# Spectral stages of a two-layer kernel: casts out of one PSUM bank put side by side on ScalarE, a tail copy moved ahead of the sums, differences split by columns, the last filter groups sent from three queues

## The chip, the cores and the metric

The kernel runs on one core of one Trainium2 chip. A core has five engines that each work through their own list of instructions in order: TensorE (PE; its weight loads are listed apart as PEld), VectorE (DVE), ScalarE (ACT), GpSimd (POOL) and SyncE (SP). They wait for each other by semaphores. Transfers (DMAs) are started by an instruction on the list of SP, ACT or POOL and then run by themselves. PSUM is the memory into which TensorE writes its sums; SBUF is the memory that all engines work in; DRAM is the chip's large memory. The metric is the device time of one execution in microseconds (us).

## The reference

A 2048 x 576 array x goes through four residual blocks, A, B, A, B. A is sliding-window attention with 32 heads; the change leaves it alone. B multiplies the two-dimensional spectrum of the normalised array by a filter:

```python
def _B_ref(x, w_r, w_i):
    B, S, D = x.shape
    X = jnp.fft.rfft2(x, axes=(-2, -1))
    W = w_r + 1j * w_i
    X = X * W
    return jnp.fft.irfft2(X, s=(S, D), axes=(-2, -1))
...
x = x + _A_ref(_layernorm(x, axis=-1), A_wqkv, A_wo)
x = x + _B_ref(_layernorm(x, axis=-1), B_w_r, B_w_i)
x = x + _A_ref(_layernorm(x, axis=-1), A_wqkv, A_wo)
x = x + _B_ref(_layernorm(x, axis=-1), B_w_r, B_w_i)
```

## The kernel before

The two B blocks are two calls of `layer_b`, called the first and the second spectral layer below. Transforms are products with constant matrices. A float32 factor is mostly written as a high and a low part of a shorter type (fp32r): ScalarE casts a PSUM tile to the high part, VectorE subtracts this from the same PSUM tile for the low part, and TensorE multiplies high by high, high by low and low by high. Each layer runs three stages, each over 16 tiles.

**Stage f, the forward transform** (lines 195 to 259; helpers in class `Out`). The last product of the attention block is made here too, since both feed TensorE: for each token tile u, `out.ahead(u)` loads the tile, turns it (lines 566 to 579) and splits it (ScalarE cast of 512 columns, line 575; VectorE subtraction, line 576; the same for a last 128 columns, lines 587 and 588), `out.unit(u)` makes 28 matmuls (line 593) and adds the residual, `out.sums(u)` takes mean and variance. `f0(u)` normalises (ScalarE `xn`, line 198), folds the row into even and odd halves and splits a 33-column tail (GpSimd, lines 200 to 208). `f1` turns the folded tile into the PSUM tile `tp`, of which there is one, with ScalarE casts `et` (line 220) and `em` (line 222) and the VectorE subtraction between them (line 221); `f2` transforms along the row (14 matmuls, line 232; cast `yh`, subtraction `yl`), `f3` along 128 of the 2048 tokens (line 243), `f4` makes sum and difference (lines 249 to 251) and writes the tile `yd` to DRAM. The order is written out by hand: an opening (lines 273 to 287), a loop over t = 1 to 10 (lines 288 to 301), and an ending (lines 303 to 314). In the opening three tiles are normalised ahead, `norm(u)` being `sums` and `f0`; in the loop's first turn two `f0` follow each other (lines 300 and 301).

**Stage g, the filter** (lines 317 to 371). 16 groups g go through `pipe`, which in step t runs `g2(t-9)`, then `g1m(t-7)`. `g1m` makes 4 matmuls (line 331), multiplies the result by the filter on VectorE (lines 337 and 338) and combines the products on GpSimd (`uv`, lines 340 and 341). `g2` makes 4 matmuls of `uv` into `pq` (line 350) and needs the sum and the difference of the two halves of `pq`: in odd groups and in group 14 ScalarE copies one half (line 355) and VectorE makes both from PSUM (lines 356 and 357); in the other groups ScalarE copies both halves (line 359), VectorE adds (line 360) and GpSimd subtracts (line 361). The result goes to DRAM (`yd`, line 366) by ScalarE's queue (even groups and the odd ones up to 7) or by SyncE's. The last stage's first two tiles, `yis[0]` and `yis[1]`, don't wait for the way through DRAM of the last groups: groups up to FG - 1 = 11 are read back from DRAM (line 365), and groups 12 to 15 are also sent straight from SBUF, 8 rows each (line 369), by SyncE's queue, those of group 15 by ScalarE's. `warm(40)` (line 372) then keeps TensorE busy with 40 matmuls that nothing reads.

**Stage i, the inverse transform** (lines 375 to 434). `pipe` runs in step t: `ly(t)` and `ld(t-3)` (loads), `i1(t-4)`, `i2(t-5)`, `im(t-3)`, `i0(t-2)`. `i0` splits a tile into a high and a low z (ScalarE line 382, VectorE line 383), `im` copies 33 columns of each to a second place (line 388 on ScalarE, line 389 on VectorE), where the third column chunk of `i1` reads them. `i1` makes 18 matmuls into the PSUM tile `pi` (line 400; the last four of the wait below read the copied columns) and splits it: `zh`, `zl` from one bank, `zm` from the next (lines 406 to 409). `i2` makes 16 matmuls into `po` (lines 420 and 424); ScalarE copies its second half (`bs`, line 427), VectorE adds the residual twice (lines 428 and 429), GpSimd adds and subtracts `bs` (lines 430 and 431), SyncE writes the rows out. In the first spectral layer the next attention block's opening runs along in this stage (`next(nxt)`).

## Time and profile before

| | us |
|---|---|
| runs shown | 1498.57, 1501.96, 1508.23 |
| median | 1501.96 |
| the profiled execution | 1499.43 |
| its span, first to last instruction | 1497.7 |
| second spectral layer, stage f, from the first turn of tile 0 to the end of the last sums | 1230 to 1356 |
| second spectral layer, stage g | 1360 to 1405 |
| second spectral layer, stage i | 1410 to 1493 |

The times on the left of a timeline row are us from the span's start. A group row gives line, engine, operation, tile written <- tiles read, shapes and count, busy us, mean ns of one, and the idle time before it with what ended it. A wait row says which instruction waited for which, the sum in us, the count, and the longest. A windows row gives for each engine the busy us and count in a stretch, then PEclk (the granted TensorE clock as a share of full), the mean busy share of the DMA engines and GB/s. A tile is listed by the place it lies in: `oroom` and `ofree` are two large SBUF areas that hold z, the turned tiles, x and `yis`. The first spectral layer stands in the trace at 490 to 752 with the same rows.

### The profile page before, as it was taken

To read this page: it belongs to the slowest core of one execution; us is meant where nothing else is said; L and a number is where in the kernel's file an instruction comes from. 1 tells how busy PE (TensorE), PEld (TensorE's weight loads), DVE (VectorE), ACT (ScalarE), POOL (GpSimd) and SP (SyncE) were. 2 spreads that over 40 slices of the span, in tenths; PEclk is the share of its full clock that TensorE was granted. 3 is DMA by queue.
4 is the path that set the end of the run, shared out by engine and by line. 5 is a ranking of instruction groups with operands and counts; after the bars stand their busy time and mean duration, and the time that the engine had idled before them with its cause. 6 is when DMAs were issued, how large, how long until landed. Compare 5 with 4: busy or idle time off the path is not lost. (4 is left out here: it accounts for less than half of the span.)

```text
span 1497.7 us, 34567 instructions
## 1 busy us (share of the span) xinstructions
PE 1413.8 (94%) x11928; PEld 1068.9 (71%) x11928; DVE 957.0 (64%) x3140; ACT 819.5 (55%) x1994; POOL 689.2 (46%) x1134
## 2 busy tenths in 40 slices
PE   7999999999999899889899999999999988999887
PEld 7976666666656799658899766666666568985686
DVE  4328777777882565566752487777777735656575
ACT  5523777777785454224454257777777844542243
POOL 2266555555565432343321954545455644324333
PEclk9999999999999999999999999999999999999999
DMA  6756556556445475757664575665554354667553
GB/s 189 201 166 212 172 179 194 179 177 177 148 133 154 127 229 187 259 192 247 217 172 93 184 220 165 167 166 159 164 156 134 101 182 157 215 211 256 175 175 127
DMA packets 203220, 266.59 MB, mean 178 GB/s; under 512 B 103918, under 2 KB 109038, under 8 KB 202214
## 3 DMA queue, kind: packets, MB, share of 16 engines
q1 hardware_dynamic: 192934, 242.23, 53.2%
q10 hardware_dynamic: 7872, 15.70, 3.1%
q0 software_dynamic: 2240, 6.45, 1.6%
q8 instruction: 96, 1.57, 0.5%
q14 instruction: 78, 0.64, 0.1%
HBM read 165.58 MB, written 101.47 MB: 178 GB/s over the span
## 5 line engine op out<-in xcount | busy, mean ns | idle before, releaser
L895 DVE CUSTOM_DVE_ANT_0 jk<-S,mask 128x384 bf16<-128x384 f32 (+2 forms) x1024 | 490.6, 529 | 112.7 <-PE E L930 61.5
L931 ACT ACTIVATE P<-E 128x384 f32<-128x384 f32 (+2 forms) x1024 | 409.0, 476 | 124.0 <-PE E L930 102.8
L933 POOL TENSOR_SCALAR_AFFINE_SELECT P<-P 128x512 f32<-128x512 f32 x256 | 163.0, 637 | 278.5 <-ACT P L931 250.5
L893 PE MATMUL S<-ks,qs 63*128 63x384 f32 (+2 forms) x1024 | 269.1, 372 | 1.0 <-DMA qs<-qk_d 0.4
L930 PE MATMUL E<-qs,ks 64*128 64x384 f32 (+2 forms) x1024 | 222.4, 373 | 4.5 <-ACT P L931 2.5
L893 PEld LDWEIGHTS S<-ks,qs 63*128 63x128 f32 x1024 | 140.8, 185 | 105.5 <-DVE m L895 73.3
L950 PE MATMUL U<-P,vq 128*19 128x128 f32 (+1 forms) x3840 | 188.7, 329 | 1.0 <-ACT us L955 1.0
L836 PE MATMUL pj<-xh,wqh 128*128 128x512 f32 x360 | 156.6, 435 | 3.1 <-ACT vt L780 1.7
L950 PEld LDWEIGHTS U<-P,vq 128*19 128x19 f32 x3840 | 95.9, 98 | 78.0 <-issue 22.7
L936 POOL TENSOR_SCALAR_AFFINE_SELECT P<-P 128x512 f32<-128x512 f32 x224 | 142.7, 637 | 0.0
L593 PE MATMUL ops<-oroom 128*128 128x288 f32 x840 | 123.5, 303 | 4.4 <-DVE oroom L576 3.0
L930 PEld LDWEIGHTS E<-qs,ks 64*128 64x128 f32 x1024 | 114.1, 185 | 18.7 <-ACT P L931 9.2
L836 PE MATMUL pj<-xh,wql 128*128 128x512 f32 x360 | 124.5, 419 | 0.4 <-POOL wql L498 0.4
L836 PE MATMUL pj<-xl,wqh 128*128 128x512 f32 x288 | 122.2, 424 | 0.0
L593 PEld LDWEIGHTS ops<-oroom 128*128 128x128 f32 x840 | 115.3, 193 | 6.2 <-DVE oroom L576 4.0
L400 PE MATMUL pi<-oroom 128*128 128x128 f32 (+1 forms) x576 | 73.7, 277 | 21.0 <-DVE oroom L389 16.1
L836 PEld LDWEIGHTS pj<-xh,wqh 128*128 128x128 f32 x360 | 67.9, 189 | 34.7 <-issue 10.6
L400 PEld LDWEIGHTS pi<-oroom 128*128 128x128 f32 (+1 forms) x576 | 68.6, 192 | 25.9 <-DVE oroom L389 20.0
L851 DVE TENSOR_TENSOR sg<-pj,sg 128x512 fp32r<-128x512 f32 x72 | 49.5, 687 | 58.4 <-ACT sg L848 58.4
L895 DVE DVE_READ_ACCUMULATOR2_ANT m<- 128x1 f32 x1024 | 85.1, 83 | 0.0
L430 POOL TENSOR_TENSOR xo<-xo,bs 128x289 f32<-128x289 f32 x32 | 25.5, 798 | 123.9 <-DVE xo L428 123.9
L836 PEld LDWEIGHTS pj<-xh,wql 128*128 128x128 f32 x360 | 64.2, 189 | 21.0 <-issue 10.7
(186 smaller groups left out, 2604.6 us busy)
## 6 DMA issues: line engine op xcount, KB each, us to landing
qk_d<-sg SPq DMA_DIRECT2D x56, 512.0 KB
qs<-qk_d SPq DMA_DIRECT2D x384, 72.0 KB
ks<-qk_d SPq DMA_DIRECT2D x348, 72.0 KB
v_d<-vt SPq DMA_DIRECT2D x32, 304.0 KB
vq<-v_d SPq DMA_DIRECT2D x16, 608.0 KB
yd<-ye SPq DMA_DIRECT2D x32, 290.0 KB
wt<-in_w SPq DMA_DIRECT2D x16, 580.0 KB
x<-ofree SPq DMA_DIRECT2D x32, 288.0 KB
```

What stands on the lines that cost most here:

```text
L400: T.matmul(o, z[:, sl, c, lo:lo + m], mo, start=k == 0, stop=k == 2)
L430: P.tensor_add(xo[:, 0:DF], xo[:, 0:DF], bs[:, 0:DF])
L593: self.nc.tensor.matmul(self.ps[u][n][:, 0:288], x, self.w[p][:, wk * D + n * 288:wk * D + n * 288 + 288], start=first and i == 0, stop=la ...
L836: T.matmul(box["ps"].rearrange("r (n p) -> r n p", n=NT) if second else box["ps"], w[:, wk], x, start=s == 0, stop=s == len(ks) - 1)
L851: V.tensor_sub(rest[:, 1], by, rest[:, 0].bitcast(F32))
L893: T.matmul(ps[:, 0:N], q[b:b + 63, pair, i * 128:i * 128 + 128], k[b:b + 63, pair, lo:hi], start=True, stop=True)
L895: V.tensor_tensor_reduce(out=jk[:, 0:N], in0=ps[:, 0:N], in1=mask[:, 384 - N:384], scale=1.0, scalar=-3e38, op0=ALU.add, op1=ALU.max, accu ...
L930: T.matmul(ps[:, 0:nq], k[b:b + 64, pair, j * 128:j * 128 + 128], q[b:b + 64, pair, j * 128:j * 128 + nq], start=True, stop=True)
L931: A.activation(p[:, hl_, 0:nq], ps[:, 0:nq], AF.Exp, scale=SC)
L933: P.affine_select(out=p[:, :, 0:128], in_=p[:, :, 0:128], pattern=[[0, 4], [1, 128]], compare_op=ALU.is_ge, fill=0.0, base=0, channel_mult ...
L936: P.affine_select(out=p[:, :, 256:384], in_=p[:, :, 256:384], pattern=[[0, 4], [-1, 128]], compare_op=ALU.is_gt, fill=0.0, base=0, channel ...
L950: T.matmul(U[32 * h:32 * h + 19, (q0 % 4) * 128:(q0 % 4) * 128 + 128 * (q1 - q0)], vts[n][:, j, h], pt[n, j][:, h, (q0 - j) * 128:(q1 - j) ...
```

## The change

In stage f the cast `em` stands ahead of VectorE's subtraction for `et`, and the cast of the last 128 columns (in `turn`) ahead of the subtraction of the first 384: ScalarE's two casts of a PSUM tile follow each other, then VectorE's two subtractions. The turn of tile 5 stands ahead of `f2(0)`, the turn of tile 6 and the sums of tile 4 ahead of the loop, and each turn of the loop normalises tile t + 3 where it normalised t + 4, so none has two. In the ending, tile 15's first 22 matmuls stand first, its last 6 after `f1(11)` and `f3(10)`, and tiles 14 and 15 are normalised earlier among the f's.

In stage g every group but 15 is done alike: ScalarE copies both halves, VectorE adds, and of the difference GpSimd makes the first 192 columns and VectorE the other 98. FG is 11, so groups 11 to 15 are sent straight. Group 14's way to DRAM goes from ScalarE's queue to SyncE's, its two straight pieces and one of group 15's to GpSimd's queue; ScalarE keeps one piece of group 15.

In stage i the tail copy is one ScalarE instruction for both parts of z and stands ahead of `i2`; the cast `zm` stands ahead of the subtraction `zl`.

```diff
@@ -130,7 +130,7 @@
 
     yd = [dram.tile([16, 16, 8, 2 * NF], F32, name=f"yd{j}") for j in range(2)]
     OPEN = *range(7, 20, 2), 20
-    FD, FG = 13, 12
+    FD, FG, SH = 13, 11, 192
     with ExitStack() as stack:
         banks, inner = ExitStack(), ExitStack()
         ip = stack.enter_context(tc.tile_pool(name="bi", bufs=1))
@@ -218,8 +218,8 @@
             em = h["em"] = wp.tile([128, 2, 128], F32R, tag="te", name=f"em{n2}", bufs=3)
             t4 = tp[:, :, 0:256].rearrange("p c (a t) -> p c a t", a=2)
             A.copy(et[:, :, 0:2], t4)
+            A.copy(em[0:99], tp[0:99, :, 256:384])
             V.tensor_sub(et[:, :, 2:4], t4, et[:, :, 0:2].bitcast(F32))
-            A.copy(em[0:99], tp[0:99, :, 256:384])
 
         def f2(n2, h):
             ps = pp.tile([128, 2, 512], F32, tag="mm", name=f"pf{n2}", bufs=3)
@@ -281,36 +281,37 @@
         out.tail(6)
         f1(0, hs[0])
         out.unit(4, pp)
+        out.ahead(5, pp)
         f2(0, hs[0])
-        out.ahead(5, pp)
         norm(3)
         out.tail(7)
+        out.ahead(6, pp)
+        out.sums(4)
         for t in range(1, NT - 5):
             u = t + 4
             out.unit(u, pp)
             f1(t, hs[t])
             f3(t - 1, hs[t - 1])
             f4(t - 1, hs[t - 1])
-            if t == 1:
-                out.ahead(6, pp)
             out.sums(u)
             f2(t, hs[t])
             out.ahead(u + 2, pp)
-            if t == 1:
-                norm(4)
-            f0(u, hs[u])
+            f0(u - 1, hs[u - 1])
 
         b = NT - 1
-        for v, f in ((b - 4, f1), (b - 5, f3), (b - 5, f4), (b - 4, f2), (b - 3, f1)):
+        ps = pp.tile([128, 2, 512], F32, tag="mm", name="opsb", bufs=3)
+        out.early(b, [ps[:, 0], ps[:, 1]])
+        for v, f in ((b - 4, f1), (b - 5, f3), (b - 1, f0), (b - 5, f4)):
             f(v, hs[v])
-        out.unit(b, pp)
+        out.late(b)
         out.sums(b)
         for z in zs:
             V.memset(z.bitcast(F32)[:, :, :, 289:320], 0.0)
         nc.sync.dma_start(ic.rearrange("p a f -> p (a f)").bitcast(F32), ic_d.rearrange("p a f -> p (a f)").bitcast(F32))
         nc.sync.dma_start(ga.rearrange("p a j c -> p (a j c)").bitcast(F32), ga_d.bitcast(F32))
-        for v, f in ((b - 2, f1), (b - 3, f2), (b - 4, f3), (b, f0), (b - 4, f4), (b - 1, f1), (b - 2, f2), (b - 3, f3), (b - 3, f4),
-                     (b, f1), (b - 1, f2), (b - 2, f3), (b - 2, f4), (b, f2), (b - 1, f3), (b - 1, f4), (b, f3), (b, f4)):
+        for v, f in ((b - 3, f1), (b - 4, f2), (b, f0), (b - 2, f1), (b - 3, f2), (b - 4, f3), (b - 4, f4),
+                     (b - 1, f1), (b - 2, f2), (b - 3, f3), (b - 3, f4), (b, f1), (b - 1, f2), (b - 2, f3), (b - 2, f4),
+                     (b, f2), (b - 1, f3), (b - 1, f4), (b, f3), (b, f4)):
             f(v, hs[v])
         warm(24)
 
@@ -351,22 +352,24 @@
 
             ye = wp.tile([128, 2, NF], F32, tag="ye", name=f"ze{g}", bufs=3) if g % 2 else eos[g // 2 % 4]
             both = ip.tile([128, 2, NF], F32, tag="both", name=f"both{g}", bufs=2)
-            if g % 2 or g == 14:
+            if g == 15:
                 A.copy(both[:, 1], pq[:, 1, 0:NF])
                 V.tensor_add(ye[:, 0], pq[:, 0, 0:NF], both[:, 1])
                 V.tensor_sub(ye[:, 1], pq[:, 0, 0:NF], both[:, 1])
             else:
                 A.copy(both, pq[:, :, 0:NF])
+                P.tensor_sub(ye[:, 1, 0:SH], both[:, 0, 0:SH], both[:, 1, 0:SH])
                 V.tensor_add(ye[:, 0], both[:, 0], both[:, 1])
-                P.tensor_sub(ye[:, 1], both[:, 0], both[:, 1])
+                V.tensor_sub(ye[:, 1, SH:NF], both[:, 0, SH:NF], both[:, 1, SH:NF])
             yef = ye.rearrange("p c f -> p (c f)")
             if g == FG + 1:
                 for n2 in range(2):
                     nc.sync.dma_start(yis[n2][0:8 * FG].rearrange("p c f -> p (c f)"), yd[1][n2, 0:FG].rearrange("g i f -> (g i) f"))
-            (nc.sync if g % 2 and g > 8 else nc.scalar).dma_start(yd[1][:, g].rearrange("n i f -> i n f"), yef)
+            (nc.scalar if g < 13 and (g < 8 or g % 2 == 0) else nc.sync).dma_start(yd[1][:, g].rearrange("n i f -> i n f"), yef)
             if g >= FG:
                 for n2 in range(2):
-                    (nc.scalar if g == 15 else nc.sync).dma_start(yis[n2][8 * g:8 * g + 8].rearrange("p c f -> p (c f)"), yef.rearrange("(i n) f -> n i f", n=16)[n2])
+                    q = nc.sync if g < 14 else P if g == 14 or n2 else nc.scalar
+                    q.dma_start(yis[n2][8 * g:8 * g + 8].rearrange("p c f -> p (c f)"), yef.rearrange("(i n) f -> n i f", n=16)[n2])
 
         pipe(16, [(9, g2), (7, g1m), (2, gw), (0, g0)])
         warm(40)
@@ -385,8 +388,7 @@
         def im(n2, h):
             z = zs[n2 % 3]
             zf = z.bitcast(F32)
-            A.copy(z[:, 0, :, 320:353], zf[:, 0, :, 256:289])
-            V.tensor_copy(z[:, 1, :, 320:353], zf[:, 1, :, 256:289])
+            A.copy(z[:, :, :, 320:353], zf[:, :, :, 256:289])
 
         def i1(n2, h):
             z = zs[n2 % 3]
@@ -404,8 +406,8 @@
             zm = h["zm"] = ip.tile([128, 2, 128], F32R, tag="zm", name=f"zm{n2}", bufs=3)
             zhf, zlf, zmf = [a.rearrange("p a b n -> p (a b n)") for a in (zh, zl)] + [zm.rearrange("p b n -> p (b n)")]
             A.copy(zhf, psf[:, 0:512])
+            A.copy(zmf[0:97], psf[0:97, 512:768])
             V.tensor_sub(zlf, psf[:, 0:512], zhf.bitcast(F32))
-            A.copy(zmf[0:97], psf[0:97, 512:768])
             V.tensor_sub(zmf[64:97], psf[64:97, 512:768], zmf.bitcast(F32)[64:97])
 
         def i2(n2, h):
@@ -431,7 +433,7 @@
             P.tensor_sub(xo[:, 575:288:-1], xo[:, 575:288:-1], bs[:, 1:288])
             nc.sync.dma_start(dstv[:, n2], xo)
 
-        pipe(NT, [(0, ly), (3, ld), (4, i1), (5, i2), (3, im), (2, i0)], lambda t: t in OPEN and nxt and next(nxt))
+        pipe(NT, [(0, ly), (3, ld), (4, i1), (3, im), (5, i2), (2, i0)], lambda t: t in OPEN and nxt and next(nxt))
         share["banks"] = pp
         if nxt:
             next(nxt)
@@ -573,10 +575,12 @@
             T.transpose(last, self.o7[:, u], self.ident)
         copy = self.nc.vector.tensor_copy if e is self.nc.vector else self.nc.scalar.copy
         copy(oT[:, 0:512], tp)
+        oL = self.oL[u % 3]
+        if last is not None:
+            self.nc.scalar.copy(oL[:, 0:128], last)
         self.nc.vector.tensor_sub(oT[:, 512:896], tp[:, 0:384], oT[:, 0:384].bitcast(F32))
-
         if last is not None:
-            self.split_last(u, last)
+            self.nc.vector.tensor_sub(oL[:, 128:256], last, oL[:, 0:128].bitcast(F32))
 
     def turn_last(self, u, tp):
         self.nc.tensor.transpose(tp, self.o7[:, u], self.ident)
```

Three places show how the instructions stand. First, VectorE in one step of stage i, second spectral layer, before; the names are those above, `oroom<-oroom` is the tail copy and `oroom<-ofree,oroom` the low part of z:

```order
L407 TENSOR_TENSOR zl_21247<-pi_21227,zh_21246 128x512
L409 TENSOR_TENSOR zm_21248<-pi_21227,zm_21248 33x256
L428 TENSOR_TENSOR xo_21270<-ofree,po_21253 128x289
L429 TENSOR_TENSOR xo_21270<-ofree,po_21253 128x287
L389 CAST oroom<-oroom 128x2x33
L383 TENSOR_TENSOR oroom<-ofree,oroom 128x2x289
```

and a step after the change (its line numbers are those of the changed file):

```order
L410 TENSOR_TENSOR zl_21092<-pi_21072,zh_21091 128x512
L411 TENSOR_TENSOR zm_21093<-pi_21072,zm_21093 33x256
L430 TENSOR_TENSOR xo_21116<-ofree,po_21099 128x289
L431 TENSOR_TENSOR xo_21116<-ofree,po_21099 128x287
L386 TENSOR_TENSOR oroom<-ofree,oroom 128x2x289
```

The tail copy has left VectorE, where it stood behind the two additions that wait for `po`. On ScalarE it stands, after the change, between `zm` and `bs`:

```order
L408 CAST zh_21424<-pi_21405 128x512
L409 CAST zm_21426<-pi_21405 97x256
L391 CAST oroom<-oroom 128x4x33
L429 COPY bs_21450<-po_21432 128x290
L385 CAST oroom<-ofree 128x2x289
```

Second, ScalarE in the first two turns of stage f's loop, second spectral layer, from the casts of a turned tile of the attention product (`oroom<-tpo`) to the cast `et` of tile 2; before:

```order
L575 CAST oroom<-tpo_19246 128x512
L587 CAST oroom<-tpo_19246 128x128
L627 ACTIVATE ofree<-ofree,eps 128x1
L198 ACTIVATE xn_19262<-ofree 128x576
L201 COPY eo_18971<-xn_19262 128x2
L627 ACTIVATE ofree<-ofree,eps 128x1
L198 ACTIVATE xn_19274<-ofree 128x576
L201 COPY eo_18973<-xn_19274 128x2
L220 CAST et_19322<-tp_19315 128x2x256
```

and after the change:

```order
L577 CAST oroom<-tpo_19250 128x512
L580 CAST oroom<-tpo_19250 128x128
L631 ACTIVATE ofree<-ofree,eps 128x1
L198 ACTIVATE xn_19263<-ofree 128x576
L201 COPY eo_18972<-xn_19263 128x2
L220 CAST et_19311<-tp_19304 128x2x256
```

One normalisation stands ahead of `et` where two stood. Third, the end of stage g on ScalarE, second spectral layer, groups 12 to 15, before:

```order
L366 DMA yd_18956<-eo_18975 8x16x580
L355 COPY both_20871<-pq_20865 128x290
L355 COPY both_20896<-pq_20891 128x290
L366 DMA yd_18956<-eo_18977 8x16x580
L355 COPY both_20909<-pq_20903 128x290
L369 DMA ofree<-ze_20908 8x580 x2
```

and after the change:

```order
L368 DMA yd_18957<-eo_18976 8x16x580
L360 COPY both_20889<-pq_20883 128x580
L360 COPY both_20913<-pq_20908 128x580
L356 COPY both_20927<-pq_20921 128x290
L372 DMA ofree<-ze_20926 8x580
```

The transfer of group 14 (`eo_18977`) no longer stands between the copies of groups 14 and 15, and one of the two straight pieces is left. GpSimd's list, which ended with the two `uv` of group 15, now ends so:

```order
L361 TENSOR_TENSOR ze_20888<-both_20889 128x192
L341 TENSOR_TENSOR uv_20905<-ofree 128x290
L342 TENSOR_TENSOR uv_20905<-p_15_20902 128x290
L361 TENSOR_TENSOR eo_18978<-both_20913 128x192
L372 DMA ofree<-eo_18978 8x580 x2
L372 DMA ofree<-ze_20926 8x580
```

Three transfers now stand behind GpSimd's last subtraction.

## Prediction

> **What bounds the kernel now.** I read the busy row first, then stretches of the second spectral layer by stage, then what TensorE's weight loads waited for, then single steps in the timeline.

> ```profile
> PE 1413.8 (94%) x11928; PEld 1068.9 (71%) x11928; DVE 957.0 (64%) x3140; ACT 819.5 (55%) x1994; POOL 689.2 (46%) x1134
> 1310.00:1345.00 35.00, 33.32 (x239) 32.25 (x238) 19.05 (x52) 16.31 (x38) 8.39 (x21) 0.95 0.60 199
> 1367.00:1402.00 35.00, 33.55 (x224) 15.99 (x222) 29.12 (x51) 7.07 (x14) 24.68 (x35) 1.00 0.69 231
> 1414.00:1498.00 84.00, 68.05 (x524) 65.84 (x524) 52.32 (x93) 31.59 (x76) 26.91 (x32) 0.95 0.48 160
> ```

> TensorE carries the kernel. Where a spectral layer leaves it idle, as in 16 of the 84 us from 1414 (stage i), a wait that goes is time gained, until another engine's work per step reaches TensorE's. In stage g (1367 to 1402) TensorE shows 33.55 of 35 us and VectorE 29.12.

> **Stage i: the tail copy leaves VectorE.** Waits of the weight loads in the first layer's stage i (first row) and in the second's; then one step of the second:

> ```profile
> PEld pi L400 <- DVE oroom L389: 10.1, 14, 1.2
> PEld pi L400 <- DVE oroom L389: 9.9, 14, 1.0
> ...
> 1431.71 0.65 DVE L389 CAST oroom<-oroom 128x66 fp32r<-128x66 f32 x1
> 1432.41 0.42 PEld L400 LDWEIGHTS pi<-oroom 128*97 128x97 f32 x4 [0.99 <-DVE oroom L389]
> ...
> 1425.37 0.41 ACT bs L427
> ...
> 1483.15 0.41 ACT bs L427
> ```

> The copy of tile n + 1 stands behind VectorE's two additions for the `po` of tile n - 1, so TensorE stops in each step until these are through. The two `bs` rows of the chain lie 12 steps apart: 57.8 / 12 = 4.82 us a step. Of that 9.9 / 14 = 0.71 is this wait; 4.11 is TensorE's own work. After the change the copy stands on ScalarE behind `zm`, about two us before it is read. What is late next? VectorE had 52.32 us over some 17 steps, 3.1 a step, and loses 0.65; ScalarE 1.9, plus at most 0.3 for a longer copy; GpSimd 1.6: all under 4.11. L383, next in VectorE's list, is read by TensorE only a step later. So the wait goes, but not in the first steps, where z comes from transfers still: I take -9 per layer of 9.9 and 10.1. Bounds: 0.71 x 14 = -10, and -5 should half come back as a wait for `zl` or `zm`, whose subtraction now stands one cast (0.37 us) later; in the first layer VectorE also works for the next attention block.

> **Stage f: order of casts, one normalisation per turn, the ending.** In the loop's steady turns the moved cast costs and saves nothing: TensorE's list has no gap there and the low part, which now comes one cast later, is read only behind the eight matmuls of the high part. At the ends, waits of the weight loads from 1231 to 1357:

> ```profile
> PEld pf L232 <- ACT et L220: 3.4, 2, 2.2
> PEld ops L593 <- DVE oroom L576: 2.0, 2, 1.5
> PEld tp L214 <- POOL tl L208: 1.6, 1, 1.6
> PEld pz L243 <- DVE yl L236: 1.4, 2, 0.8
> PEld tpo L570 <- ACT em L222: 1.2, 1, 1.2
> PEld ops L593 <- ACT oroom L575: 0.9, 1, 0.9
> ```

> The order shows a remedy for each but the 1.5 of L576, which lies before the loop, and the 0.6 of L236 at the very end. `et` came behind two normalisations, now one; `f0(15)`, which makes `tl`, stands ahead of `f1(13)` where it stood behind `f3(11)`, with two tiles' f1, f2 and f3 before its reader; the turn of tile 6 has 2 us of `f2(0)` between it and the turn of tile 5. Gone: 3.4 + 0.5 + 1.6 + 0.8 + 1.2 + 0.9 = 8.4. New: the turn of tile 5 needs `tp` as soon as unit 4 ends:

> ```profile
> 1238.12 3.74 PEld L593 LDWEIGHTS ops<-oroom 128*128 128x128 f32 x28
> 1241.32 0.58 ACT L220 CAST et<-tp 128x512 fp32r<-128x512 f32 x1
> 1241.94 0.69 DVE L221 TENSOR_TENSOR et<-tp,et 128x512 fp32r<-128x512 f32 x1 [1.65 <-ACT et L220]
> 1242.66 0.37 ACT L222 CAST em<-tp 99x256 fp32r<-99x256 f32 x1 [0.76 <-DVE et L221]
> ```

> `tp` is free at 1241.90 + 0.37 + 0.69 = 1243.0 and TensorE is there at 1241.9: 1.1 us. Net -7 per layer. Bounds: -4, if half of the ending's waits come back, and -9, as the PEclk of 0.95 from 1310 to 1345 says 0.05 x 35 = 1.75 us go to a slower clock behind the ending's gaps.

> **Stage g: differences split.** Weight loads of `pq` in the second layer, four groups, and the instructions of one pair:

> ```profile
> 1372.27 0.79 PEld L350 LDWEIGHTS pq<-uv,m 64*128 64x128 f32 x8 [0.44 <-issue]
> 1374.58 0.79 PEld L350 LDWEIGHTS pq<-uv,m 64*128 64x128 f32 x8 [0.44 <-POOL uv L340]
> 1384.52 0.79 PEld L350 LDWEIGHTS pq<-uv,m 64*128 64x128 f32 x8 [0.44 <-issue]
> 1386.66 0.46 DVE L360 TENSOR_TENSOR eo<-both 128x290 f32<-128x290 f32 x1
> 1386.68 0.99 POOL L341 TENSOR_TENSOR uv<-p 128x290 f32<-128x290 f32 x1
> 1389.03 0.40 ACT L355 COPY both<-pq 128x290 f32<-128x290 f32 x1 [2.41 <-POOL uv L340]
> 1389.54 0.79 PEld L350 LDWEIGHTS pq<-uv,m 64*128 64x128 f32 x8 [0.44 <-issue]
> ...
> L360 DVE TENSOR_TENSOR eo<-both 128x290 f32<-128x290 f32 x7 | 4.1, 580 | 2.4 <-ACT both L359 2.3
> L389 DVE CAST oroom<-oroom 128x66 fp32r<-128x66 f32 x16 | 9.5, 591 | 0.1
> ...
> 1387.04 0.75 DVE L337 TENSOR_TENSOR ofree<-p,wt 128x580 f32<-128x580 f32 x1
> 1387.71 0.75 DVE L338 TENSOR_TENSOR p<-p,wt 128x580 f32<-128x580 f32 x1
> ```

> A group costs TensorE 2.31 (1372.27 to 1374.58) and takes 5.02 / 2 = 2.51 (1384.52 to 1389.54). At best 14 x 0.20 = -2.8 per layer. But each group now has two VectorE instructions that read SBUF alone beside GpSimd's three, and the rows show what such neighbours do: L360 began at 1386.66 and the `uv` beside it took 0.99. The short subtraction of 98 columns isn't in this trace; the nearest is L389, 591 ns mean. With L360's mean of 580 and twice 0.68 for L337 and L338 (they start 1387.71 - 1387.04 = 0.67 apart) a group costs VectorE 0.58 + 0.59 + 1.36 = 2.53, what it takes now: 0. Upper bound, all at their longest: 0.99 + 0.65 + 1.36 = 3.00, 15 x 0.49 = +7 per layer.

> [...]

> **From g to i: three queues.**

> ```profile
> 1403.04 5.37 PEld L265 LDWEIGHTS warm<-dc 128*128 128x128 f32 x40 [0.39 <-issue]
> 1403.43 0.58 ACTq L366 DMA_DIRECT2D yd<-eo  x1
> 1404.11 0.40 ACT L355 COPY both<-pq 128x290 f32<-128x290 f32 x1 [2.92 <-DMA yd<-eo]
> 1405.40 2.21 ACTq L369 DMA_DIRECT2D ofree<-ze  x2
> 1409.79 0.67 ACT L382 CAST oroom<-ofree 128x578 fp32r<-128x578 f32 x1 [5.27 <-DMA ofree<-ze]
> 1412.31 0.68 ACT L382 CAST oroom<-ofree 128x578 fp32r<-128x578 f32 x1 [0.77 <-DMA ofree<-ze]
> 1416.00:1419.50 3.50, 3.50 (x18) 3.50 (x18) 1.88 (x3) 0.99 (x3) 0.00 (x0) 0.50 1.00 373
> 1412.60:1416.00 3.40, 3.29 (x19) 3.11 (x18) 2.08 (x4) 2.13 (x5) 0.00 (x0) 0.54 0.77 186
> ks<-qk_d POOLq DMA_DIRECT2D x36, 72.0 KB, 3.7
> ```

> Group 15's copy waited behind the transfer of group 14 on ScalarE's list until 1404.11; `pq` was done a little after 1403.0. So tile 0 comes 1 us sooner. Tile 1's piece went second on ScalarE's queue and landed 2.5 us after tile 0's; from GpSimd at 3.7 us it lands with it, and TensorE spends 2 us on tile 0 before it needs it. Group 14's two pieces now go by GpSimd from about 1402.4 and, at 3.7 and with a us between them, land at 1406 to 1407, under the cover of group 15's until 1408.8. If GpSimd's transfers took 3 us more, that cover is gone and tile 0 is late by some 2. The clock was half from 1412.6 to 1419.5 (PEclk 0.54 and 0.50), costing 0.46 x 3.4 + 0.50 x 3.5 = 3.3 us, behind a pause of 2 us after the warming matmuls; a pause 1 us shorter may spare it. I take 1.0 plus half of 3.3: -2.5. Bounds -5 and +3.

> [...]

> **The sum.** Per layer -9 - 7 + 0 - 2.5 = -18.5, twice -37. The profiled execution took 1499.4 us (span 1497.7 and 1.7 around it); 1499.4 - 37 = 1462.4. The median of the runs, 1502.0, lies 2.6 above that execution, within their spread of 10.

> **Rivals.**
> - *The port in stage g.* All collisions at their longest: +7 per layer, 1462.4 + 14 = 1476. For it: 0.99 us beside 0.46. Against: L360's mean is 0.58, and GpSimd's share shrinks from 290 to 192 columns.
> - *Stage i gives half.* -5 per layer and not -9: 1462.4 + 8 = 1470. For it: zl and zm later, the first layer's extra VectorE work. Against: 2 us between them and their matmuls.
> - *The f waits only change place:* 1462.4 + 14 = 1476. Against: tile 15 gets 9 us.
> - *Slower: stage g in single file.* ScalarE's copy waits for its transfer's start, this for GpSimd's subtraction, this for `uv`, this for VectorE. Now this ring spans two groups. If it closed over one: copy 0.64, add 0.99, short one 0.65, two products 1.36, `uv` 0.99, subtraction 0.70, start 0.58, together 5.9 a group, +3.4 x 30 = +102, 1564. It decides from 37 / 30 = 1.2 us a group. Against: the lists keep two groups between `g1m` and `g2`.

> **How the numbers follow.** The forecast 0.63, the port 0.16, half of i 0.12, f elsewhere 0.05, single file 0.04. The forecast's own range is 1449 to 1473 (i to -10, f to -9, clock kept; or g +3 and GpSimd's transfers late). With the port and half of i, the range of 8 in 10 is 1447 to 1480. A measurement here tells about 1% (15 us) from no change. Faster by more than that needs under 1485 on the profiled execution: the first four cases but for a tail, where two of them meet: 0.88. Within 1%: 0.08. Slower: 0.04.

> **What would show it.** Right: no weight load of L400 waits for VectorE, and the `bs` rows lie 4.1 us apart; the six f rows shrink to about 3.2 in all; the `pq` loads stay near 2.5 apart; the first cast of z comes under 6.5 us behind group 15's copy. Wrong: `bs` still 4.5 or more apart, `pq` 2.8 or more, or the first z waiting for a GpSimd transfer.

## The result and the profile after

The changed kernel took 1480.5 us (median of 4 runs, 1479.9 to 1482.4) against 1501.8 for the kernel before (4 runs, 1498.6 to 1508.2), a ratio of 0.986 with an interval of 0.982 to 0.989. The gain is 21 us where 37 were forecast, and the time lies just above the range. The profiled execution took 1479.9 us (span 1478.1), 19.5 less than the one before.

The busy row of the page of the changed kernel:

```profile
PE 1402.8 (95%) x11928; PEld 1061.4 (72%) x11928; DVE 960.7 (65%) x3122; ACT 817.3 (55%) x1994; POOL 705.1 (48%) x1156
```

The same three stretches as in the prediction (end of f, g, i of the second layer), shifted to where they now lie; the columns are length, busy time of TensorE, weight loads, VectorE, ScalarE, GpSimd, granted clock, DMA share and GB/s:

```profile
1295.60:1330.60 35.00, 32.28 (x245) 31.34 (x245) 21.27 (x58) 18.14 (x43) 14.54 (x34) 1.00 0.61 205
1357.60:1392.60 35.00, 30.20 (x194) 13.19 (x190) 33.04 (x51) 8.28 (x13) 26.10 (x38) 1.00 0.62 199
1404.00:1478.00 74.00, 65.20 (x527) 64.78 (x526) 46.60 (x78) 31.28 (x77) 30.02 (x32) 0.94 0.54 178
```

The middle row is the news. In stage g TensorE fell from 33.55 to 30.20 us of 35 and VectorE rose from 29.12 to 33.04: it is now the busiest engine there. Stage i needs 74 us for what took 84.

**Stage i.** What its weight loads wait for, two rows of the first layer and then two of the second, and one step on the timeline:

```profile
PEld pi L402 <- ACT oroom L385: 3.3, 1, 3.3
PEld pi L402 <- ACT oroom L391: 1.7, 2, 0.9
...
PEld pi L402 <- ACT oroom L391: 1.7, 2, 0.9
PEld pi L402 <- ACT oroom L385: 1.7, 1, 1.7
```

```profile
1415.64 0.40 ACT L429 COPY bs<-po 128x290 f32<-128x290 f32 x1 [1.13 <-PE po L426]
...
1418.19 0.32 ACT L391 CAST oroom<-oroom 128x132 fp32r<-128x132 f32 x1
1418.34 0.69 DVE L410 TENSOR_TENSOR zl<-pi,zh 128x512 fp32r<-128x512 f32 x1 [0.23 <-ACT zm L409]
...
1419.34 1.96 PEld L402 LDWEIGHTS pi<-oroom 128*128 128x128 f32 x18
1419.68 0.40 ACT L429 COPY bs<-po 128x290 f32<-128x290 f32 x1 [1.16 <-PE po L426]
...
1423.68 0.40 ACT L429 COPY bs<-po 128x290 f32<-128x290 f32 x1 [1.13 <-PE po L426]
```

No load waits for VectorE any more. The tail copy (L391) stands over a microsecond ahead of the loads that read it, and the `bs` copies lie 4.04 and 4.00 us apart where they lay 4.82. What is left are the first tiles, which come from transfers.

**Stage f.** Weight loads from 1216 to 1342:

```profile
PEld tp L214 <- issue: 2.7, 1, 2.7
PEld tp L214 <- ACT oroom L580: 1.9, 1, 1.9
PEld ops L597 <- DVE oroom L581: 1.5, 1, 1.5
PEld tpo L572 <- DVE et L222: 1.1, 1, 1.1
...
PEld pz L243 <- DVE yl L236: 0.6, 1, 0.6
PEld tp L214 <- POOL tl L208: 0.4, 1, 0.4
```

The rows that should stay (1.5, 1.1, 0.6) are there and make the 3.2 forecast. Two that no step of the prediction had are there too: 2.7 and 1.9. The 2.7 is put down to "issue"; VectorE's list shows what is behind it:

```profile
1321.99 0.46 DVE L250 TENSOR_TENSOR ye<-pz,half 128x290 f32<-128x290 f32 x1 [1.52 <-ACT half L249]
...
1322.73 0.81 DVE L619 TENSOR_TENSOR ofree<-ofree,opsb 128x288 f32<-128x288 f32 x2
1323.45 0.81 DVE L626 BATCH_NORM_STATS2 ofree<-ofree 128x6 f32<-128x288 f32 x2
1324.30 0.21 DVE L627 BATCH_NORM_AGGREGATE ofree<-ofree 128x2 f32<-128x12 f32 x1
1324.49 0.43 DVE L309 MEMSET oroom<- 128x124 f32 x3
1324.84 0.63 DVE L222 TENSOR_TENSOR et<-tp,et 128x512 fp32r<-128x512 f32 x1
```

`f1(13)` needs the bank `tp` that `f1(12)` filled, and the last reader of that bank (L222 at 1324.84) stands in VectorE's list behind the sums of `f4(10)`, `late(15)`'s additions, the statistics of tile 15 and three memsets. The 1.9 is tile 6's turn: its two casts stand on ScalarE behind `f0(3)`, and `f1(1)` waits for the bank.

**Stage g.** One group of the second layer:

```profile
1368.02 0.75 DVE L338 TENSOR_TENSOR ofree<-p,wt 128x580 f32<-128x580 f32 x1
1368.17 0.59 ACTq L368 DMA_DIRECT2D yd<-ze  x1
1368.69 0.74 DVE L339 TENSOR_TENSOR p<-p,wt 128x580 f32<-128x580 f32 x1
...
1368.85 0.64 ACT L360 COPY both<-pq 128x580 f32<-128x580 f32 x1 [2.30 <-DVE ofree L338]
1369.51 0.69 POOL L342 TENSOR_TENSOR uv<-p 128x290 f32<-128x290 f32 x1
1369.53 1.00 DVE L362 TENSOR_TENSOR eo<-both 128x290 f32<-128x290 f32 x1
...
1370.16 0.74 POOL L361 TENSOR_TENSOR eo<-both 128x192 f32<-128x192 f32 x1
...
1370.45 0.58 DVE L363 TENSOR_TENSOR eo<-both 128x98 f32<-128x98 f32 x1
...
1370.95 0.75 DVE L338 TENSOR_TENSOR ofree<-p,wt 128x580 f32<-128x580 f32 x1
1371.10 0.58 ACTq L368 DMA_DIRECT2D yd<-eo  x1
...
1371.77 0.64 ACT L360 COPY both<-pq 128x580 f32<-128x580 f32 x1 [2.28 <-DVE ofree L338]
```

It is 2.93 us from one L338 to the next: 1.51 for two products, 0.92 for the sum, 0.50 for the 98 columns (start to start). The sum begins just after a `uv` on GpSimd and takes 1.00 where a like one took 0.46 before; the piece begins inside GpSimd's subtraction.

VectorE is idle for only 0.10 us of this, between the end of the second product (1369.43) and the sum, which starts 0.04 behind the end of the copy that it reads. That copy starts 0.09 behind the end of ScalarE's transfer start for the group before (1368.17 + 0.59), and a transfer start comes 0.07 behind the end of the piece (1370.45 + 0.58, then 1371.10). The row puts the copy's wait down to L338, but the copy at 1379.92, with no transfer start ahead of it, begins before such a product (1379.75 + 0.75) ends. So a ring over one group closes as well: start to copy 0.68, copy to sum 0.68, sum to piece 0.92, piece to the next start 0.65, together the same 2.93. Where SyncE starts the transfer, as for group 9, the next copy comes earlier (1379.92), the sum begins ahead of the `uv` (1381.09 and 1381.25) and takes 0.50, GpSimd's `uv` pays with 0.90, and the group takes 2.44 (L338 at 1379.75 and 1382.19).

**From g to i**, the copy of group 15, the straight pieces and the first cast:

```profile
1393.79 0.40 ACT L356 COPY both<-pq 128x290 f32<-128x290 f32 x1 [2.41 <-PE pq L351]
...
1395.08 0.61 ACTq L372 DMA_DIRECT2D ofree<-ze  x1
1395.35 0.54 POOL L372 DMA_DIRECT2D ofree<-ze  x1 [0.50 <-DVE ze L358]
1400.11 0.67 ACT L385 CAST oroom<-ofree 128x578 fp32r<-128x578 f32 x1 [5.92 <-DMA ofree<-ze]
...
1401.82 0.67 ACT L385 CAST oroom<-ofree 128x578 fp32r<-128x578 f32 x1
```

The copy now follows the last `pq` at once, and tile 1 follows tile 0 by 1.71 us, not 2.5. But the first cast comes 6.3 us behind the copy where it came 5.7 behind it (in the first layer 7.9 and 5.5): the piece on ScalarE's queue landed later.

**The table of stages.** From the first and last starts in each trace: f is the first `xn` to the last subtraction of f4, g the first `p` load to the last `pq` load, i the first cast of z to GpSimd's last subtraction; two values are the two layers. "Lost" is the sum of (1 - granted clock) x length over stretches of 2 us in f and in i.

| kernel | f | lost | g | g to i | i | lost |
|---|---|---|---|---|---|---|
| before | 122.7, 122.8 | 2.8, 2.9 | 42.6, 42.5 | 7.8, 7.3 | 82.2, 82.1 | 3.4, 3.4 |
| changed | 119.9, 117.1 | 3.4, 0.0 | 47.3, 47.5 | 8.7, 7.0 | 73.1, 71.7 | 5.1, 3.4 |

Over both layers f gave 8.5 and i 19.5; g took 9.7, the way from g to i 0.6 and that from f to g 0.4: -17.3. The other 2.3 of the 19.6 by which the span fell lie ahead of, between and behind these stages (the first layer's f begins 4.2 us sooner, the second attention block is 1.4 longer, the tail 0.5). The 4.2 are no gain of the change: in the run with the queues alone, whose stage f is the one of before, f begins at 488.6, in the changed kernel at 488.2 and in the kernel before at 492.4.

### The profile page after: what moved, and what is told of

Its sections match the earlier page's. It is cut to its first block, busy times and chain, and to the rows that moved or that the text cites. A ratio compares the mean times of both kernels' runs of the same rounds, so it can differ in the third digit from the quotient of the medians.

```text
span 1478.1 us, 34753 instructions
## 1 busy us (share of the span) xinstructions
PE 1402.8 (95%) x11928; PEld 1061.4 (72%) x11928; DVE 960.7 (65%) x3122; ACT 817.3 (55%) x1994; POOL 705.1 (48%) x1156
## 4 chain that ended last, share of the span: by engine, by line
PE 71%; DMA 7%; ACT 5%; DVE 4%; POOL 3%; issue 3%; ACTq 1%; SPq 1%; POOLq 0%; DVEq 0%
PE pj L840 16%; PE S L897 11%; PE U L954 10%; PE ops L597 6%; PE E L934 5%; PE pi L402 4%; PE vps L780 4%; PE pf L232 4%; PE po L422 3%; PE tpo L968 2%; ACT P L935 2%; PE pz L243 1%; DMA yd<-ye 1%; DMA ofree<-yd 1%; PE po L426 1%
## 5 line engine op out<-in xcount | busy, mean ns | idle before, releaser
L935 ACT ACTIVATE P<-E 128x384 f32<-128x384 f32 (+2 forms) x1024 | 409.0, 477 | 122.8 <-PE E L934 100.0
L597 PE MATMUL ops<-oroom 128*128 128x288 f32 x784 | 114.0, 302 | 2.5 <-DVE oroom L581 2.5
L597 PEld LDWEIGHTS ops<-oroom 128*128 128x128 f32 x784 | 106.8, 191 | 3.4 <-DVE oroom L581 3.0
L840 PEld LDWEIGHTS pj<-xh,wql 128*128 128x128 f32 x360 | 64.2, 189 | 21.0 <-issue 10.8
L852 ACT CAST sg<-pj 128x512 fp32r<-128x512 f32 x72 | 42.1, 585 | 62.3 <-PE pj L840 47.8
L402 PE MATMUL pi<-oroom 128*128 128x128 f32 (+1 forms) x576 | 69.2, 277 | 7.4 <-ACT oroom L385 4.6
```

The lines of the kernel that those rows point to most:

```text
L402: T.matmul(o, z[:, sl, c, lo:lo + m], mo, start=k == 0, stop=k == 2)
L597: self.nc.tensor.matmul(self.ps[u][n][:, 0:288], x, self.w[p][:, wk * D + n * 288:wk * D + n * 288 + 288], start=first and i == 0, stop=la ...
L840: T.matmul(box["ps"].rearrange("r (n p) -> r n p", n=NT) if second else box["ps"], w[:, wk], x, start=s == 0, stop=s == len(ks) - 1)
L935: A.activation(p[:, hl_, 0:nq], ps[:, 0:nq], AF.Exp, scale=SC)
```

## The experiments

The theory after the result, named "port theory" in the expectations: stage g lost what it lost because VectorE's two instructions with both operands in SBUF collide with GpSimd's, so that one of a pair takes longer (1.00 where a like one took 0.46). A port is in no trace; what the runs show is how long each instruction takes beside the other. The rivals: the ring of ScalarE's copies and transfer starts; the new queues. A second question was why f gave less than 7 per layer.

### Stage g: sums and differences in five other kernels

The first takes back the old sums in the changed kernel:

```diff
-            if g == 15:
+            if g % 2 or g == 14:
...
-                P.tensor_sub(ye[:, 1, 0:SH], both[:, 0, 0:SH], both[:, 1, 0:SH])
                 V.tensor_add(ye[:, 0], both[:, 0], both[:, 1])
-                V.tensor_sub(ye[:, 1, SH:NF], both[:, 0, SH:NF], both[:, 1, SH:NF])
+                P.tensor_sub(ye[:, 1], both[:, 0], both[:, 1])
```

> The changed kernel with the sums and differences of stage g as they were before (odd groups and 14: half a copy, both sums from PSUM on VectorE; even groups: whole copy, sum on VectorE, whole difference on GpSimd); queues and FG stay as changed. Port theory (VectorE's two SBUF-only instructions of each group meet GpSimd's three, stage g is 4.7 and 5.0 us longer than before): both layers give that back, 1480.5 - 9.7 = 1471. Rival (the loss comes from the new queues: transfer starts on ScalarE's list hold up its copies): the time stays at 1480 +- 2 and stage g at 47 us.

Measured: 1475.1 us (1472.4 to 1478.5, 5 runs), stage g 42.9 and 42.4. The loss is in the sums; the new queues, which stayed, have no part in it. In the median 5.4 of the expected 9.7 came back (6.6, if each kernel is compared with its own runs of before); in the profiled execution 7.5.

The second makes every group as group 15:

```diff
-            if g == 15:
+            if g >= 0:
                 A.copy(both[:, 1], pq[:, 1, 0:NF])
```

> The changed kernel with every group of stage g done as group 15: ScalarE copies one half, VectorE adds and subtracts straight from PSUM, so no VectorE instruction there reads SBUF alone and GpSimd has only its two uv instructions. Port theory: VectorE costs 0.46 + 0.45 + 2 x 0.68 = 2.27 us a group, less than TensorE's 2.31; the period falls from 2.7 to 2.9 to about 2.35, stage g to about 41 us, 1480.5 - 2 x 6.5 = 1467 to 1468. Rival (the ring of copy, uv and transfer start sets the period, not the port): stage g no shorter than the 42.5 of before, 1471 or more.

Measured: 1462.1 us (1458.3 to 1469.8, 6 runs), ratio 0.973 (0.970 to 0.976); stage g 40.3 and 40.6. The rival falls: without SBUF-only work on VectorE the ring does not hold stage g at the 42.5 of before. The ring is shorter there, too (a copy of 0.40, sums of 0.46 and 0.45), so this run does not tell how much of the changed kernel's loss came by way of it.

The third takes the 98 columns from VectorE and gives GpSimd the whole difference:

```diff
-                P.tensor_sub(ye[:, 1, 0:SH], both[:, 0, 0:SH], both[:, 1, 0:SH])
+                P.tensor_sub(ye[:, 1], both[:, 0], both[:, 1])
...
-                V.tensor_sub(ye[:, 1, SH:NF], both[:, 0, SH:NF], both[:, 1, SH:NF])
```

> The changed kernel with the whole difference of groups 0 to 14 on GpSimd (no 98-column piece on VectorE). Port theory in the form that every SBUF-only instruction of the two engines takes the port alone in turn: per group VectorE 0.46 and GpSimd 0.70 + 0.70 + 0.74 make 2.60 of port time beside 2.56 (0.46 + 0.16 + 0.70 + 0.70 + 0.54) in the changed kernel: no better than 1480 +- 4. Rival (VectorE's length alone counts, 1.00 + 0.58 + 1.49 = 3.07 falls to 2.45): stage g back at 42 to 43, about 1471.

Measured: 1472.4 us (1467.1 to 1481.5, 6 runs), stage g 42.6 and 42.4. The theory in its strict form falls. Three rows of this kernel, and the sum of the next group:

```profile
1352.58 0.70 POOL L342 TENSOR_TENSOR uv<-p 128x290 f32<-128x290 f32 x1
...
1353.11 0.49 DVE L362 TENSOR_TENSOR eo<-both 128x290 f32<-128x290 f32 x1 [0.61 <-ACT both L360]
1353.24 0.92 POOL L361 TENSOR_TENSOR eo<-both 128x290 f32<-128x290 f32 x1
...
1355.53 0.50 DVE L362 TENSOR_TENSOR ze<-both 128x290 f32<-128x290 f32 x1 [0.59 <-ACT both L360]
```

A group takes 2.42 us, less than the 2.60 that the strict form adds up. The sum now comes late in GpSimd's `uv` and takes 0.49; GpSimd's difference, which begins ahead of the sum's end, takes 0.92 (a like one 0.70 in the median before) and pays. What counts is what waits for the one that pays: VectorE is now idle for 0.6 us a group, in which it waits for ScalarE's copy, and the copy stands behind the start of the transfer that waits for GpSimd's difference (its end at 1354.16, the start at 1354.19, the copy at 1354.86, the next sum at 1355.53).

The fourth is the split alone in the kernel before:

```diff
-            if g % 2 or g == 14:
+            if g == 15:
...
-                P.tensor_sub(ye[:, 1], both[:, 0], both[:, 1])
+                P.tensor_sub(ye[:, 1, 0:SH], both[:, 0, 0:SH], both[:, 1, 0:SH])
+                V.tensor_sub(ye[:, 1, SH:NF], both[:, 0, SH:NF], both[:, 1, SH:NF])
```

> The kernel before with nothing but the split differences of stage g (192 columns on GpSimd, 98 on VectorE, the sum on VectorE from the copy, groups 0 to 14); old queues, old FG, old stages f and i. Port theory: stage g 4.7 to 5.0 us longer in each layer, 1501.8 + 9.7 = 1511. Rival (new queues cost it): 1502 +- 3.

Measured: 1510.0 us (12 runs) against 1503.0, ratio 1.0048 (1.0020 to 1.0076); stage g 47.2 and 46.9. By itself this part makes the kernel slower, by half a percent.

The last of this group changes only where an operand lies. Instructions, their sizes and GpSimd's share stay:

```diff
-                V.tensor_add(ye[:, 0], both[:, 0], both[:, 1])
-                V.tensor_sub(ye[:, 1, SH:NF], both[:, 0, SH:NF], both[:, 1, SH:NF])
+                V.tensor_add(ye[:, 0], pq[:, 0, 0:NF], both[:, 1])
+                V.tensor_sub(ye[:, 1, SH:NF], pq[:, 0, SH:NF], both[:, 1, SH:NF])
```

> The changed kernel where VectorE's sum and its 98-column piece take their first operand from PSUM (pq) and not from ScalarE's copy; instructions, lengths and GpSimd's share stay. Port theory (a VectorE instruction with both operands in SBUF takes turns with GpSimd's, one with an operand in PSUM does not): the sum falls from 0.73 to 0.80 (mean) to 0.46, the piece from 0.6 to 0.65 to about 0.2, GpSimd's uv stay 0.70; VectorE costs 2.0 us a group and stage g falls to 41 to 42.5 as TensorE or the ring of copy, sum and transfer allows: about 1470. Rival (they are long for another reason, as their place behind the products): they stay at 0.7 and 0.6, stage g at 47, 1480.

Measured: 1465.2 us (1459.8 to 1468.9), ratio 0.976 (0.972 to 0.980); stage g 40.4 and 40.1. One group:

```profile
1356.24 0.70 POOL L342 TENSOR_TENSOR uv<-p 128x290 f32<-128x290 f32 x1
1356.50 0.46 DVE L362 TENSOR_TENSOR ze<-pq,both 128x290 f32<-128x290 f32 x1 [0.34 <-ACT both L360]
...
1356.88 0.25 DVE L363 TENSOR_TENSOR ze<-pq,both 128x98 f32<-128x98 f32 x1
1356.90 0.53 POOL L361 TENSOR_TENSOR ze<-both 128x192 f32<-128x192 f32 x1
```

The sum runs beside the same `uv` and takes 0.46, not 1.00; the piece takes 0.25, not 0.58; GpSimd's subtraction 0.53, not 0.74. Nothing but the operand's place changed, so the collision in SBUF is shown to be what made these instructions long. That their length then counts by way of VectorE's list and of the ring is read from the rows; no run has all of stage g's transfers started by SyncE, which would part the two.

### The other parts alone

Stage i's part in the kernel before:

```diff
-            A.copy(z[:, 0, :, 320:353], zf[:, 0, :, 256:289])
-            V.tensor_copy(z[:, 1, :, 320:353], zf[:, 1, :, 256:289])
+            A.copy(z[:, :, :, 320:353], zf[:, :, :, 256:289])
...
+            A.copy(zmf[0:97], psf[0:97, 512:768])
             V.tensor_sub(zlf, psf[:, 0:512], zhf.bitcast(F32))
-            A.copy(zmf[0:97], psf[0:97, 512:768])
...
-        pipe(NT, [(0, ly), (3, ld), (4, i1), (5, i2), (3, im), (2, i0)]
+        pipe(NT, [(0, ly), (3, ld), (4, i1), (3, im), (5, i2), (2, i0)]
```

> The kernel before with stage i's part alone (whole tail copy on ScalarE ahead of the additions, zm cast ahead of zl's subtraction). Theory: the predicted step holds by itself, stage i 82.2 to about 72, 1502.5 - 2 x 10 = 1482 to 1483. Rival (part of it came from the queues, which bring the first tiles in earlier, or from stage g): stage i 75 or more, 1487 or more.

Measured: 1479.2 us against 1500.6, ratio 0.985 (0.979 to 0.991); stage i 73.4 and 74.4, of which the clock lost 5.1 and 6.8. This part alone is worth the whole change.

Stage f's part in the kernel before (order of casts, loop, turn and ending as in the change's diff, of which these are the lines that count most here):

```diff
-            f0(u, hs[u])
+            f0(u - 1, hs[u - 1])
...
-        out.unit(b, pp)
+        out.late(b)
```

> The kernel before with stage f's part alone (order of casts, one normalisation per turn, the new ending). Theory: stage f 122.8 to between 117.1 and 119.9, depending on whether the clock falls at the ending, 1502.5 - 6 to - 11 = 1492 to 1497. Rival (waits only change place): 122 or more, 1501 or more.

Measured: 1492.6 us (10 runs) against 1500.6, ratio 0.995 (0.992 to 0.997); stage f 121.2 and 119.8, with 4.5 and 3.4 lost to the clock. The waits are those of the changed kernel (2.7, 1.9, 1.5, 1.1).

The queues alone:

```diff
-    FD, FG = 13, 12
+    FD, FG = 13, 11
...
-            (nc.sync if g % 2 and g > 8 else nc.scalar).dma_start(yd[1][:, g].rearrange("n i f -> i n f"), yef)
+            (nc.scalar if g < 13 and (g < 8 or g % 2 == 0) else nc.sync).dma_start(yd[1][:, g].rearrange("n i f -> i n f"), yef)
             if g >= FG:
                 for n2 in range(2):
-                    (nc.scalar if g == 15 else nc.sync).dma_start(yis[n2][8 * g:8 * g + 8].rearrange("p c f -> p (c f)"), yef.rearrange("(i n) f -> n i f", n=16)[n2])
+                    q = nc.sync if g < 14 else P if g == 14 or n2 else nc.scalar
+                    q.dma_start(yis[n2][8 * g:8 * g + 8].rearrange("p c f -> p (c f)"), yef.rearrange("(i n) f -> n i f", n=16)[n2])
```

> The kernel before with the last groups' queues and FG = 11 alone. Theory from the changed kernel's trace (the piece on ScalarE's queue lands later when GpSimd's go beside it, the second tile earlier): g to i within 1 us of the 7.3 and 7.8 of before, time 1502 +- 2. Rival (the prediction's term): 2.5 us less per layer, 1497.5.

Measured: 1501.6 us (10 runs), ratio 1.0006 (0.998 to 1.003); g to i 9.2 and 7.2. The queues brought nothing that shows. The four parts alone, each against its own runs of before, make +7.0 - 21.4 - 8.0 + 1.1 = -21.3, as the whole change did (-21.4); with intervals of plus or minus 4 to 9 us on each part, so close an agreement is in part luck.

### The ending of f, the opening, and the clock

The changed kernel with the ending of f in another order:

> The changed kernel with the ending of stage f in another order: f4(10) ahead of f0(14), f1(12) directly behind late(15), the sums of tile 15 behind f1(12), the three memsets of z behind f1(13). Theory: the 2.7 us for which TensorE stands before f1(13) come from f1(12)'s subtraction standing on VectorE behind late(15)'s additions, the sums and the memsets; gone, stage f falls from 117.1 (second layer, clock full) to about 114.5 and a fall of the clock behind that pause goes too: 1480.5 - 5.4 to - 8 = 1473 to 1475. Rival (the wait is for f0(14) and f4(10) on ScalarE, or only moves to f1(14)): under 1 us per layer, 1479 or more.

```diff
-        for v, f in ((b - 4, f1), (b - 5, f3), (b - 1, f0), (b - 5, f4)):
+        for v, f in ((b - 4, f1), (b - 5, f3), (b - 5, f4), (b - 1, f0)):
             f(v, hs[v])
         out.late(b)
+        f1(b - 3, hs[b - 3])
         out.sums(b)
+        f2(b - 4, hs[b - 4])
+        f0(b, hs[b])
+        f1(b - 2, hs[b - 2])
         for z in zs:
             V.memset(z.bitcast(F32)[:, :, :, 289:320], 0.0)
...
-        for v, f in ((b - 3, f1), (b - 4, f2), (b, f0), (b - 2, f1), (b - 3, f2), (b - 4, f3), (b - 4, f4),
+        for v, f in ((b - 3, f2), (b - 4, f3), (b - 4, f4),
```

Measured: 1479.0 us (4 runs; the changed kernel took 1480.5), stage f 117.9 and 119.1 with 1.4 and 2.7 lost, so 116.5 and 116.4 without. The 2.7 is gone from the list, and this stands there instead:

```profile
PEld tp L214 <- POOL eo L202: 2.3, 2, 1.2
```

The rival holds: `f0(14)` and `f0(15)` come later, and GpSimd's part of them is late next. The following kernel (on the one with every group from PSUM) leaves `f0(14)` where it was:

> The kernel with every group of stage g done from PSUM (1462.1 in its runs, stage f 119.6 and 119.7 with the clock fallen at the ending) and in stage f only the sums of tile 15 and the memsets of z moved behind f1(12) and behind the last f4; f0(14) keeps its place ahead of f4(10). Theory: f1(12)'s subtraction starts 1.35 us sooner, the wait before f1(13) falls from 2.7 to about 1.3, and the clock stays: stage f about 115.7 to 116, 1462.1 - 2 x 3.7 = 1455. Rival (the wait moves to another tile as it did with f0(14) late): stage f 117 or more, 1458 or more.

Measured: 1464.8 us (1458.1 to 1468.3), stage f 118.2 and 116.7, with 1.6 and 0.0 lost. The edit is

```diff
         out.late(b)
+        f1(b - 3, hs[b - 3])
         out.sums(b)
-        for z in zs:
-            V.memset(z.bitcast(F32)[:, :, :, 289:320], 0.0)
...
-        for v, f in ((b - 3, f1), (b - 4, f2), (b, f0), (b - 2, f1), (b - 3, f2), (b - 4, f3), (b - 4, f4),
+        for v, f in ((b - 4, f2), (b, f0), (b - 2, f1), (b - 3, f2), (b - 4, f3), (b - 4, f4),
...
+        for z in zs:
+            V.memset(z.bitcast(F32)[:, :, :, 289:320], 0.0)
         warm(24)
```

and the wait moved again; these rows stand for the 2.7:

```profile
PEld tp L214 <- POOL tl L208: 1.8, 2, 1.4
...
PEld tp L214 <- POOL eo L202: 1.2, 1, 1.2
```

Longer warming between g and i:

```diff
-        warm(40)
+        warm(56)
```

> The same kernel (every group from PSUM, 1462.1) with 56 warming matmuls between stages g and i instead of 40, 16 x 0.143 = 2.3 us more on TensorE, which ends about when the first z is cast. Theory (the half clock at stage i's start follows from the pause of 2.1 us behind the 40): no half clock there, stage i up to 3.3 us shorter per layer, 1462.1 - 6 = 1456. Rival (the later pauses of 0.7 between the first tiles bring the half clock anyway, or the warming matmuls end too late): 1462 +- 2.

Measured: 1461.0 us (1459.6 to 1463.6), the same within the spread. Stage i is 70.7 and 69.1 with 1.7 and 0.0 lost, where the kernel with 40 had 71.9 and 73.3 with 3.4 and 5.1 lost. This is more than the chance of one execution: the 24 layers with 40 in the profiles of the other kernels lost 3.4 to 6.8 in stage i, the four with 56 (this kernel and the next) 0.0 to 1.7. The second layer at 40 warming matmuls and then at 56, granted clock third from the end:

```profile
1391.00:1395.00 4.00, 3.67 (x18) 3.68 (x19) 1.88 (x3) 1.11 (x4) 0.00 (x0) 0.50 0.96 348
...
1388.00:1392.00 4.00, 4.00 (x36) 4.00 (x35) 2.21 (x5) 1.94 (x6) 0.00 (x0) 1.00 0.95 334
```

Last, all of these and the opening, where tile 6's turn goes ahead of `f0(3)`:

```diff
+        out.ahead(6, pp)
         norm(3)
         out.tail(7)
-        out.ahead(6, pp)
```

> Every group from PSUM, the new ending of stage f, 56 warming matmuls, and at the opening of stage f the turn of tile 6 ahead of f0(3). Theory: the three gains add, -3.7 - 3 - 1.5 per layer, 1462.1 - 16 = 1446. Rival (the opening's wait only moves, the clock falls elsewhere): as the better of the two others, 1455.

Measured: 1456.2 us (1448.5, 1450.1, 1462.2 and 1464.6), ratio 0.972 (0.967 to 0.977). The wait of 1.9 is gone from the opening without another in its place: without the clock's loss f is 114.8 and 115.0, against 116.6 and 116.7 in the kernel with the ending alone. It is the best median of all, but its runs do not tell it from the kernel that only takes every group from PSUM (0.973). That kernel already beats both the kernel before and the changed one.

## Why the prediction was wrong

**Stage i (-9 per layer) was right:** 9.1 and 10.4 less, without the clock's loss 10.8 and 10.4. The wait was the one named, and nothing came in its place but the first tiles.

**Stage g (0) is the step that failed.** The prediction took 0.58 us for VectorE's sum, the mean of L360 in the kernel before, and 0.59 for the piece. There the sum stood in seven groups of sixteen, and in the pair that was quoted it began at 1386.66, just ahead of the `uv` at 1386.68, so that GpSimd paid with 0.99. Its mean says nothing of a list in which it always follows the second product, which is just when GpSimd begins the second `uv`. It measured 0.73 to 0.80 in the mean and 1.00 in the steady groups. Of the 0.40 us by which a steady group exceeds the 2.53 of the prediction, the sum makes 0.34 (0.92 start to start) and the time behind the second product 0.16 (0.84, not 0.68, as the sum waits for the copy); the piece, at 0.50, gives 0.09 back. The sign that the prediction had named for being wrong came: the `pq` loads lie 2.92 apart (1369.60 and 1372.52). The rival with all collisions at their longest had the sign, and with it the sum is 14 us longer by its price; +4.7 and +5.0 per layer were paid. No run shows the port after which that rival is named; the runs show lengths. The row that should have decided was quoted: 0.99 beside 0.46. In the rows of the changed kernel the one that starts second takes longer (`uv` at 1369.51 with 0.69, the sum at 1369.53 with 1.00; the sum at 1381.09 with 0.50, `uv` at 1381.25 with 0.90), but for one pair in each layer whose starts all but coincide (in the second `uv` at 1361.08 with 1.02, the sum at 1361.09 with 0.46); once an operand lies in PSUM, the sum takes 0.46 beside a `uv` of 0.70 that started first. A sum of lengths is too strict all the same, as the 2.42 us of the third kernel show against 2.60, and there the sum that began 0.17 ahead of the end of a `uv` took 0.49, only 0.03 more than undisturbed.

**Stage f (-7) was mis-sized:** 2.8 and 5.7 less. The difference of the two is the clock. Without it f fell from 119.9 to 116.5 and 117.1: some 3 us. The 8.4 of old waits went but for 0.4 of the 1.6 for `tl`; the step that failed is the list of new ones, 1.1 in the prediction against 1.1 + 2.7 + 1.9 in the trace. It asked of each moved piece whether its reader is in time, and not whose bank it holds: both new waits are for the single bank `tp`, whose last reader stands behind other work on its own engine. The time lies between the forecast and "f elsewhere", given 1 in 20.

**From g to i (-2.5):** +0.9 and -0.3. The copy did come about 1 us sooner, but the piece landed later, and the half clock stayed (granted 0.50 from 1404 to 1408). From the issue of group 15's piece for tile 0 on ScalarE's queue to the first cast it took 4.2 and 4.4 us before and 6.7 and 5.0 after; GpSimd's pieces took 4.5 and 5.4 us to land (medians of groups 14 and 15) where the prediction took 3.7. What made the piece later is open: in the profiles of the two kernels with the memsets behind the last f4 the first cast came 5.4 to 5.8 us behind the last `pq` in both layers, in the others with the same three queues 6.6 to 9.2.

**The sum:** -18.5 was forecast per layer; i at -9.75 and f at -4.25 in the mean make -14.0, and g with the ways to and from it gives back 5.35: -8.65. In the profiled execution, 17.5 us above the forecast of 1462.4, g makes 9.7 of the miss, the way from g to i 5.6 and f 5.5; i and the parts outside the stages gave 1.5 and 2.3 more than forecast. A half of stage i did not show, nor the single file of 5.9 us a group. But a shorter ring did close over one group, that of copy, sum, piece and transfer start (2.93). The distance of two groups between `g1m` and `g2` does not open it, since all four stand in `g2`.

## What to carry to other kernels

An instruction's price is that of its neighbours in time: before work on SBUF alone goes to VectorE beside GpSimd, look what GpSimd runs at that very moment in the new order, and take the price from the row with such a neighbour (here 1.00 us), not from a mean (0.58). If VectorE can take one operand from PSUM beside GpSimd, let it: here that made the same arithmetic half as long (0.46 for 1.00 us, 0.25 for 0.58). When an order is changed, ask of each step whose buffer it waits for and what stands ahead of that buffer's last reader on its engine; and ask of each transfer start what it waits for and which instruction of the next step stands behind it on the same list.

## What the runs showed of the hardware

The clock's loss comes in pieces. In all 14 traces each stretch at half clock (granted 0.50) lasts one to four times 3.41 us, except the last, which the kernel's end cuts off; half clock for 3.41 us loses 1.7. The starts of these stretches lie whole multiples of 3.413 us apart in each trace; in the changed kernel they are 488.6, 591.0, 669.5, 867.5, 1403.4 and 1475.1.

Whether a pause costs a piece goes with where it lies on this grid, of which a window is here one length of 3.413 us. In stage f of five kernels with the same code of that stage (the changed one and four with other sums in g) the loss in a layer was 0.0 five times, 1.1, 1.2, and 3.3 to 3.4 three times. The same pause of 2.7 us stands in all ten layers, and half clock followed it only in the three that lost 3.3 to 3.4; the rest of the loss is a piece at the opening. In stage i of all kernels the loss was 0.0, 1.7, 3.4, 5.1 or 6.3 to 6.8. The first and second layer of the changed kernel, at the same place behind the same pause:

```profile
588.00:592.00 4.00, 1.47 (x9) 1.27 (x8) 3.71 (x13) 1.17 (x4) 1.14 (x4) 0.87 0.58 165
592.00:596.00 4.00, 4.00 (x24) 4.00 (x23) 0.69 (x1) 2.33 (x5) 2.26 (x5) 0.70 0.87 306
...
1321.00:1325.00 4.00, 2.08 (x16) 1.84 (x14) 2.98 (x11) 2.62 (x7) 2.26 (x5) 1.00 0.23 53
1325.00:1329.00 4.00, 3.39 (x26) 3.35 (x26) 2.00 (x5) 2.42 (x5) 1.56 (x2) 1.00 0.84 268
```

Ahead of some pieces stood only pauses shorter than a window: TensorE stood for 2.53 us up to 591.00, where a piece at half clock begins in the changed kernel, and for 1.88 us up to 1410.51 in the kernel before, where one begins at 1412.88.
